# A table that also picks the engine of each copy, cast and sum, with forty SBUF sums on GpSimd

## The chip, the cores and the metric

The kernel runs on one core of a Trainium2 chip. The time is that of the device, in microseconds (us), from the start of the launch to its end; lower is better. Each version is run several times and the median is its time. A profile shows one execution. In it PE is the matrix engine (PEld is its loading of weights), DVE the vector engine, ACT the scalar engine, POOL is GpSimd, and SP is the engine that issues most of the DMAs (its queue is written SPq).

## The reference, cut to what matters

For 8 batches of 8 heads, 576 positions and 64 columns a head:

```python
def phi(x, c, s):
    r = np.maximum(x, 0.0)
    return np.concatenate([r * c, r * s], axis=-1)   # c, s: cos and sin of the position
q_p, k_p = phi(q, cos_w, sin_w), phi(k, cos_w, sin_w)
kv = np.einsum('bhsf,bhsd->bhfd', k_p, v)
z = np.sum(k_p, axis=2)
num = np.einsum('bhsf,bhfd->bhsd', q_p, kv)
den = np.einsum('bhsf,bhf->bhs', q_p, z)[..., None] + 1e-06
x = (num / den)            # heads side by side: 4608 rows of 512
h = x @ w_in               # 512 x 2048
g = h * np.cos(h)
out = g @ w_out            # 2048 x 512
```

All inputs and the output are float32; inside, the kernel computes its matrix products on float16 operands and sums them in float32.

## The kernel before, in words

**Work.** The 576 positions of a batch are handled as 512 rows plus a rest of 64. The eight 512-row parts and a ninth chunk made of the eight rests go through the two layers as nine chunks (`c` = 0 to 8). For each batch the attention stage runs: `load` brings k, q and v (two DMAs each from SP's queue); `prep` makes the cosine and sine features of q and k from float32 data in SBUF (`KQ<-km`, `KQ<-qm`, L452 on ACT, L453 on DVE); `cast_v` rounds v to float16 (`V<-vm`, L466 on ACT, L467 on DVE, L468 on POOL); `kv` multiplies (`ATT<-V,KQ`, L479) and copies the result to `kvz`; `num` multiplies with q (L542) and divides (L566, L568) into `x16`; and x is turned over into `xT`, by matrix products and a copy (`x_pe`, L588, L593) for the first three batches and by a transposing DMA (`x_dma`, L599) for the others. q is turned over in the same two ways (`q_pe`, L509, L514, L516, and `q_dma`, L520).

**Layers.** `layer1` computes h in PSUM banks, and `gate` evicts it: ACT takes the cosine (`ch<-M`, L609), DVE multiplies it with h into `gT` (L614). `layer2` makes the output rows in `ost`, which `store` writes out. From chunk 3 on part of layer 1, and from chunk 1 on all of layer 2, use a block scheme with seven half-size products in place of eight. That scheme needs **sums and differences of float16 blocks that lie in SBUF**: of the weights (`w_in_sums`, `WS`, L717; `w_out_sums`, `T`, L904), of x (`layer1_sums`, `XS`, L738) and of g (`layer2`, `S2`, `S3` and two updates in place of `gT`, L926 and L979). Its copies out of PSUM are `seed` (L663, bank to bank), `copy` in `layer1_fast` (`Z<-M`, L789), `copy` in `layer2` (`ost<-M`, L959) and one in `layer2_plain` (L889). In `layer1_fast` the gate of two blocks at once is a 1024-wide product of two float32 operands in SBUF (`gT<-Z,ch`, L808).

**Order.** Every operation is a step of `Plan`, with an engine, a cost, and the buffers that it reads and writes. The order in which each engine's steps stand is set by a list scheduler (`forward`) that takes one number per step from the table `KEYS`; the numbers are keys of order, not times. Steps with several possible engines (`either`: the features, the casts of v from batch 2 on, `den`) take the engine that is free first in the scheduler's account. Steps marked `port=True` on DVE and all on POOL are kept apart there. On the chip only data dependencies (semaphores) order the engines against each other.

**Start.** SP loads q, k and v of batch 0. POOL waits for k with a tiny cast (`hold`, L1027), then issues four DMAs for `w_in` (512 columns of the 2048 each, cast to float16 on the way), then those for `w_out`. The loads of batch 1 are held back: `hold_raw` (L1052) writes one element of each raw tile from an element of `w_in_sb`, named by `GATE1`, so that SP's load of k waits until that quarter of `w_in` has landed. `warm` (L1022) are products without use that keep PE's clock up while data are on the way.

Of the kernel before, what the change touches and what calls it, by code (L numbers as in the profile page):

```python
# [10 lines left out]
AF = mybir.ActivationFunctionType  # L11
# [6 lines left out]
    5824, 5995, 5824, 2967, 2673, 126, 143, -359, -2881, 263, -1072, -2121, 539, -49, 2962,  # L18
    2726, 3623, 3679, 1739, 3937, 2137, -2208, -6512, 4069, -2017, 702, -6077, -768, 703, -754,
    -6331, 8159, 3076, -1894, -5732, 1581, -6769, -1234, -877, -673, -882, -751, -1585, -1235,  # L20
    617, -63, -2524, -424, -626, 4458, 1519, -1459, -1432, 1518, -1601, 1517, -828, -5827,
    -6392, 1404, 4308, -2500, 2020, -1958, -2107, -3266, -4898, 8136, -5552, -8420, -2791,
    -1468, -4655, -1451, -1052, 783, -6576, 2792, -3465, -355, -8421, -3123, 6479, -3015, -6472,
    -1591, -2075, -2619, -2729, -7369, -6796, 3263, 798, -2481, 6480, -2003, -7073, 6781, 423,
    1982, 1241, 120, -9188, 1380, 643, -11779, -6829, 9984, -8175, -7566, 1246, -8162, 512,
    -312, -11302, 511, 10443, -10259, 2437, 605, 4807, 1897, 5905, -9831, -5057, 9984, 2301,
    -5301, 8846, -10101, -6662, 9020, -11634, -568, 7671, 5055, -1712, 6604, 584, 1196, 5001,
    -1672, 2279, 3129, 2596, 3289, 895, 532, -4417, -5551, -4542, 2044, 1687, 2846, 2800, 1902,
    3378, 993, -5427, 6673, -5442, 8455, 6488, 5906, 5871, 7397, -1850, 7157, -1228, 5182, 5994,
    7349, -880, 4039, 6762, 7533, 1736, 4177, 11737, 11954, 7479, 6368, 6930, 8684, 7392, 5307,  # L30
    17180, 16483, 5398, 7497, -1619, 7409, 8721, -161, 1062, -838, 10292, 5065, 5035, 7002,
    2938, 4999, 14973, 16942, 5320, 7491, 5034, 4630, 11782, 14974, 11886, 4631, 7315, 4601,
    4503, -692, -956, 4504, 7814, 2937, 3132, -860, 16897, -3069, -418, 10427, 3570, 3895, 4526,
    811, 1495, 8147, 4216, 8205, 4347, 7685, 6163, 8521, 4575, 8538, 4733, 3460, 8421, 9350,
    4611, 8493, 5428, 5849, 9131, 9146, 7933, 8134, 4534, 8052, 5570, 6030, 5703, 3236, 9273,
    5079, 7033, 7959, -732, 8555, 4350, -5307, 8046, 8768, 11196, 7765, 7621, 12926, 8253, 8411,
    11956, 11554, 8883, 13897, 9078, 9732, 12216, 1417, 8512, 13854, 7780, 9806, 6177, 5415,
    9049, -520, 5974, 11813, -2437, 5998, 8827, 10404, 7711, 13087, 3521, 9257, 1171, 1138,
    4633, 11805, 2569, 2323, 2261, 2582, 5745, 6182, 8706, 9578, 5077, 10082, 8860, -990, 8453,
    8541, 6221, 8499, 9036, 12232, 10067, 9664, 8544, 14012, 6360, 6188, 8015, 4438, -1489,  # L40
    6985, 8390, 5805, 5879, 5943, 6028, 8049, 8537, 10462, 5198, 8396, 8395, 12558, 4688, 9262,
    6122, 9046, 8189, 3466, 1589, 7820, 11893, 7819, 12664, 3857, 3643, 11985, 9433, 9054, 9210,
    8708, 8410, 9843, 8144, 4689, 8846, 8992, 9753, 8959, 11174, 12280, 10511, 11156, 9526,
    5553, 7072, 10317, 10402, 10261, 8357, 10403, 10051, 10267, 14404, 18351, 12204, 11240,
    9232, 9255, 18421, 14144, 12777, 11783, 7045, 11215, 9090, 7849, 7075, 9381, 10740, 5609,
    9483, 3041, 12189, 10009, 6763, 11687, 7171, 11186, 8968, 9229, 5228, 8069, 10107, 13655,
    8182, 10208, 13199, 8613, 9303, 15205, 7902, 9952, 15535, 6395, 9744, 4204, 6896, 8110,
    15935, 5192, 9656, 15578, 5752, 11091, 9533, 7831, 11765, 13714, 4074, 11936, 4217, 2177,
    4612, 7204, 2638, 7978, 7784, 4545, 8636, 6647, 6639, 5918, 8225, 3758, 5656, 6600, 8239,
    8692, 9382, 5468, 10740, 10372, 5666, 8703, 3916, 8802, 9066, 9050, 9298, 9304, 4801, 9527,  # L50
    9521, 8286, 11521, 9621, 9449, 6022, 5622, 9514, 9669, 10572, 6135, 8767, 7485, 8972, 9413,
    9995, 4213, 8900, 10075, 9675, 10273, 6234, 14794, 10195, 8079, 8885, 4804, 11145, 9576,
    11000, 9480, 10532, 11021, 11980, 10074, 11419, 13188, 13339, 10446, 11020, 12065, 12937,
    12270, 12793, 12994, 13467, 14479, 13933, 13146, 11684, 12054, 13603, 13106, 11695, 11512,
    14005, 13771, 13161, 15965, 16177, 16249, 16753, 13045, 12409, 18114, 13650, 12372, 12951,
    11343, 17252, 18836, 11725, 9919, 9604, 12293, 15415, 7956, 11448, 14519, 12454, 13519,
    14769, 15313, 12053, 13106, 13257, 13105, 13291, 11473, 11759, 13416, 11450, 13716, 18849,
    11925, 12834, 16093, 13478, 14576, 16431, 12255, 12362, 15960, 13160, 14519, 15910, 14407,
    11420, 14173, 9926, 10508, 15133, 9344, 13280, 12367, 9947, 9788, 14407, 10518, 12980,
    11697, 11766, 15535, 11429, 11430, 11395, 14648, 15418, 12373, 10069, 8755, 10521, 8003,  # L60
    11441, 13572, 10404, 12329, 17053, 10754, 11091, 10405, 4849, 9215, 7332, 8545, 10442, 9859,
    10283, 8824, 11855, 11042, 10408, 9428, 9240, 10089, 6840, 10015, 11937, 13432, 12329,
    14986, 8570, 13601, 11278, 9846, 10850, 12123, 10120, 9231, 12906, 11502, 11095, 17486,
    13263, 10990, 10503, 12334, 12434, 12727, 10556, 12848, 11321, 12810, 13349, 12759, 11144,
    9468, 12544, 13893, 13417, 10912, 9663, 12457, 8909, 13137, 14576, 14577, 13435, 14151,
    10310, 14092, 13571, 10884, 9832, 16768, 15657, 11596, 15684, 17182, 16270, 13098, 17070,
    15987, 15606, 6694, 19176, 16271, 6282, 21578, 15029, 12700, 14864, 23503, 25176, 13602,
    15549, 15974, 10832, 14466, 16061, 14589, 10209, 12007, 14031, 13538, 17903, 15093, 14046,
    16754, 11592, 18103, 14972, 15838, 14550, 15534, 14971, 15051, 13097, 12823, 12047, 14361,
    15045, 11016, 15607, 13066, 17291, 15370, 14684, 17730, 15344, 15696, 14507, 15369, 21381,  # L70
    12422, 13612, 16306, 16082, 6980, 15110, 25709, 16196, 6566, 16377, 16411, 13784, 6718,
    14056, 16929, 17039, 16412, 6717, 14282, 13875, 16186, 15098, 22414, 15303, 22094, 16880,
    22547, 17762, 13257, 17979, 16921, 14246, 17264, 11458, 9954, 12478, 12363, 11239, 12491,
    14328, 14703, 14327, 12412, 12275, 11391, 10099, 13674, 8800, 17476, 13817, 17651, 13961,
    11696, 6628, 12348, 11074, 13449, 15450, 13381, 15669, 12970, 15927, 14201, 13093, 13364,
    12833, 18387, 16087, 14472, 14480, 15193, 14959, 15363, 15351, 15446, 6483, 6363, 15673,
    13288, 19922, 16059, 5627, 15685, 13188, 12766, 16307, 5411, 15687, 15666, 15185, 16308,
    22136, 16271, 16582, 24827, 15769, 13994, 13943, 25782, 17223, 13256, 21089, 14718, 11697,
    19012, 23721, 13825, 12713, 16047, 27330, 19676, 26392, 12356, 19171, 19137, 25153, 20300,
    24575, 20816, 24148, 19933, 18704, 24601, 25241, 17614, 17642, 17213, 18192, 16667, 17540,  # L80
    17171, 17978, 15747, 16040, 12652, 16869, 17381, 18358, 12108, 26009, 16442, 15097, 18968,
    22506, 14325, 14468, 23722, 18748, 14353, 20959, 15309, 13207, 22948, 15406, 18806, 26434,
    17307, 19122, 13503, 14496, 16600, 16449, 18225, 17438, 15143, 16606, 15242, 16591, 19935,
    16631, 20110, 9977, 20151, 16345, 17596, 21986, 16007, 17814, 13492, 12529, 20878, 14542,
    9673, 17980, 17287, 16452, 14758, 16015, 17852, 17506, 19481, 13918, 17894, 12836, 13589,
    13910, 13566, 13751, 13668, 14062, 15321, 15434, 16469, 13488, 16029, 15409, 14091, 15728,
    14680, 15600, 16039, 16251, 16182, 25040, 25175, 15758, 15758, 15924, 19149, 16297, 17009,
    15666, 18342, 17524, 13007, 17309, 17010, 16166, 17102, 17420, 15086, 22399, 17317, 15221,
    17973, 25853, 16870, 21058, 13956, 17170, 22819, 13269, 14811, 19018, 17792, 25500, 20349,
    16959, 18873, 20325, 20305, 21587, 16184, 24900, 24202, 15971, 17496, 19642, 20403, 16741,  # L90
    21754, 22533, 22239, 10620, 21802, 21987, 17248, 21696, 21441, 23431, 22029, 23368, 17736,
# [1107 lines left out]
```

## Time and profile before

| | before |
|---|---|
| median of 3 runs | 285.55 us (285.11, 286.81, 285.55) |
| the profiled execution | 284.34 us, of which 282.3 us are its span, first to last instruction |
| granted PE clock | 0.993 |
| PE busy | 270.5 us, 2715 products |
| DVE busy | 249.2 us, 443 instructions |
| ACT busy | 218.0 us, 396 instructions |
| POOL busy | 19.2 us, 32 instructions |

"Busy" of PE covers the pipelined products from start to modelled end, so that a busy PE is not a proof that none was late; the distance from one start to the next tells that. The chain of waits lists, in order of time, what ran on the path that ended last: start, length, engine, tile, line and count. A line of the timeline gives start, length, engine, line, operation, tiles, shapes and count, and in brackets the idle time before it and what ended it. A line of the groups ends with count, busy time and mean nanoseconds of one.

### The profile page before, as it was taken

The numbers are of one execution on the slowest core, as the hardware profiler recorded it, in microseconds if no ns is written. First come the engines' busy times: TensorE is split into PE (matmuls) and PEld (weight loads), VectorE is DVE, ScalarE is ACT, GpSimd is POOL, SyncE is SP. The second block draws the span as 40 slices with busy tenths as digits, with TensorE's granted clock in tenths as the row PEclk, the third lists the DMA queues.
The fourth block names the chain that finished last, engine by engine and source line by source line (L and its number), as shares of the span: only waits on it lengthen the run. The fifth ranks groups of instructions, "written<-read, shape, count | busy, mean of one in ns | idle before, by whom it ended". The sixth has DMA issues, their size and how long they took to land.

```text
span 282.3 us, 6870 instructions
## 1 busy us (share of the span) xinstructions
PE 270.5 (96%) x2715; PEld 219.1 (78%) x2715; DVE 249.2 (88%) x443; ACT 218.0 (77%) x396; POOL 19.2 (7%) x32
## 2 busy tenths in 40 slices
PE   7799988999989999999999999999999999999994
PEld 2668956678967667779787988898788888888883
DVE  2877796999999989998999999999999999997952
ACT  2856698896899998599899999996676675877420
POOL 1440020010000010003003000210000000000000
PEclk9799999999999999999999999999999999999999
DMA  6999999969979999997999899988013100300124
GB/s 204 312 200 222 298 291 267 320 133 285 311 231 235 211 229 293 241 310 161 308 234 268 167 275 270 240 117 251 3 37 116 57 2 0 151 0 2 74 77 149
DMA packets 77599, 53.30 MB, mean 189 GB/s; under 512 B 46080, under 2 KB 75264, under 8 KB 77568
## 3 DMA queue, kind: packets, MB, share of 16 engines
q1 hardware_dynamic: 72608, 48.12, 66.7%
q0 software_dynamic: 4224, 4.19, 9.5%
q10 hardware_dynamic: 736, 0.57, 0.6%
q8 instruction: 21, 0.34, 0.5%
q14 instruction: 10, 0.08, 0.1%
HBM read 36.74 MB, written 9.44 MB: 164 GB/s over the span
## 4 chain that ended last, share of the span: by engine, by line
PE 85%; DVE 5%; DMA 4%; ACT 3%; issue 1%; DVEq 0%
PE M L948 32%; PE M L780 15%; PE M L637 10%; PE M L677 7%; PE TR L780 6%; PE M L880 5%; PE ATT L542 3%; DMA xT<-x 2%; PE ATT L479 2%; DMA qm<-in_q_dram 2%; PE M L509 2%; PE ATT L1022 1%; PE TR L677 1%; DVE x L568 1%; ACT xT L593 1%; ACT KQ L452 1%
## 5 line engine op out<-in xcount | busy, mean ns | idle before, releaser
L609 ACT ACTIVATE ch<-M 128x512 f32<-128x512 f32 x90 | 53.3, 597 | 14.4 <-PE M L637 6.9
L614 DVE TENSOR_TENSOR gT<-M,ch 128x512 f16<-128x512 f32 x84 | 56.7, 685 | 5.0 <-ACT ch L609 4.6
L948 PEld LDWEIGHTS <-gT 128*128 128x128 f16 x560 | 54.0, 98 | 7.6 <-DVE gT L926 0.5
L948 PE MATMUL M<-w_out_sb,gT 128*128 128x256 f16 x448 | 55.9, 273 | 0.0
L452 ACT ACTIVATE KQ<-km,CS 128x512 f16<-128x512 f32 x55 | 37.2, 715 | 0.2 <-DMA km<-in_k_dram 0.2
L452 ACT ACTIVATE KQ<-qm,CS 128x512 f16<-128x512 f32 x47 | 32.3, 721 | 4.5 <-DMA qm<-in_q_dram 4.5
L780 PEld LDWEIGHTS <-w_in_sb 128*128 128x128 f16 x320 | 30.8, 98 | 4.3 <-issue 0.2
L948 PE MATMUL M<-T,S 128*128 128x256 f16 x256 | 32.4, 273 | 0.0
L637 PE MATMUL M<-xT,w_in_sb 128*128 128x256 f16 x256 | 30.2, 273 | 0.1
L677 PE MATMUL M<-xT,w_in_sb 128*128 128x512 f16 x112 | 27.6, 379 | 0.8 <-ACT xT L593 0.8
L948 PEld LDWEIGHTS <-S 128*128 128x128 f16 x256 | 24.7, 98 | 4.0 <-issue 0.2
L637 PEld LDWEIGHTS <-w_in_sb 128*128 128x128 f16 x256 | 24.5, 98 | 3.5 <-issue 0.4
L568 DVE TENSOR_TENSOR x<-ATT,rec 128x512 f16<-128x512 f32 x32 | 22.1, 692 | 2.3
L959 ACT ACTIVATE ost<-M 128x512 f32<-128x512 f32 x24 | 14.1, 593 | 12.1 <-PE M L948 9.3
L780 PEld LDWEIGHTS <-WS 128*128 128x128 f16 x216 | 20.5, 98 | 3.3 <-issue 0.5
L677 PEld LDWEIGHTS <-w_in_sb 128*128 128x128 f16 x128 | 12.2, 98 | 10.8 <-issue 0.9
L453 DVE TENSOR_SCALAR KQ<-qm,CS 128x512 f16<-128x512 f32 x33 | 15.4, 498 | 5.1 <-DMA qm<-in_q_dram 5.1
L468 POOL CAST V<-vm 128x1024 f16<-128x1024 f32 (+1 forms) x11 | 10.7, 1004 | 134.9 <-PE M L948 46.0
L542 PEld LDWEIGHTS <-qT 128*128 128x128 f16 x320 | 15.3, 98 | 4.6 <-issue 1.8
L926 DVE TENSOR_TENSOR S<-gT 128x2048 f16<-128x2048 f16 (+1 forms) x16 | 17.4, 1085 | 0.2
L808 DVE TENSOR_TENSOR gT<-Z,ch 128x1024 f16<-128x1024 f32 x13 | 15.9, 1221 | 0.7 <-ACT ch L802 0.4
L542 PE MATMUL ATT<-kvz,qT 128*128 128x65 f16 x288 | 15.7, 194 | 0.6 <-DVE x L568 0.5
(135 smaller groups left out, 461.3 us busy)
## 6 DMA issues: line engine op xcount, KB each, us to landing
out_dram<-ost SPq DMA_DIRECT2D x33, 256.0 KB, 3.0
qm<-in_q_dram SPq DMA_DIRECT2D x8, 640.0 KB, 5.9
km<-in_k_dram SPq DMA_DIRECT2D x8, 640.0 KB, 5.6
qm<-in_q_dram SPq DMA_DIRECT2D x8, 512.0 KB, 6.2
km<-in_k_dram SPq DMA_DIRECT2D x8, 512.0 KB, 5.7
vm<-in_v_dram SPq DMA_DIRECT2D x6, 640.0 KB, 7.2
vm<-in_v_dram SPq DMA_DIRECT2D x6, 512.0 KB, 6.5
w_in_sb<-in_moe_w_in_dram POOLq DMA_DIRECT2D x4, 512.0 KB, 8.9
```

What stands on the lines that cost most here:

```text
L452: fn = {"ACT": lambda: nc.scalar.activation(out=out_, in_=in_, func=AF.Relu, scale=sc), "DVE": lambda: nc.vector.tensor_scalar(out=out_, i ...
L453: "DVE": lambda: nc.vector.tensor_scalar(out=out_, in0=in_, scalar1=0.0, scalar2=sc, op0=ALU.max, op1=ALU.mult)}
L542: nc.tensor.matmul(bank[hb][:, hh * D1:(hh + 1) * D1], lhsT=a[:, h, :], rhs=z[:, h, :], start=(i == 0), stop=(i == len(parts) - 1))
L568: nc.vector.tensor_tensor(out=split(x16[n][:, hs, :], k), in0=A[:, :, :, 0:D], in1=split(rec[n][:, hs], k).unsqueeze(3).broadcast_to((P, k ...
L609: act(0.5, due, lambda: nc.scalar.activation(out=ch[c], in_=bank, func=AF.Sin, bias=math.pi / 2.0, scale=1.0), [key], [("ch", c)])
L614: dve(0.61, due, lambda: nc.vector.tensor_tensor(out=dst, in0=a, in1=b, op=ALU.mult), [key, ("ch", c), *rd], dkeys)
L637: nc.tensor.matmul(M1[m][:, jj * 2 * P:(jj + 1) * 2 * P], lhsT=w_in_sb[:, cc, j * P:(j + 1) * P], rhs=X[:, cc, ts], start=(cc == 0), stop= ...
L677: nc.tensor.matmul(M, lhsT=w_in_sb[:, cc, j * P:(j + 1) * P], rhs=X[:, cc, :], start=(cc == 0), stop=(cc == NCT - 1))
L780: nc.tensor.matmul(bank[0][:, j * TH:(j + 1) * TH], lhsT=a(cc, j), rhs=b[:, cc, :], start=(first and j == 0 and cc == 0), stop=(last and j ...
L808: dve(1.14, due, lambda: nc.vector.tensor_tensor(out=g4, in0=four(uz), in1=four(cc2), op=ALU.mult), zk + ck, [("g", gi(c), h * JH + j, t) ...
L926: dve(0.07 + 1.07 / NG, due, lambda: nc.vector.tensor_tensor(out=out_[:, sl], in0=a[:, sl], in1=b[:, sl], op=op), rd, wr, port=True)
L948: nc.tensor.matmul(bank[0][:, tt * MH:(tt + 1) * MH], lhsT=a[:, j, tt * P:(tt + 1) * P], rhs=b[:, j, :], start=(first and (apart or tt == ...
```

## The change

Each entry of `KEYS` now carries two things: the last digit picks the engine of the step (0: as before, the one free first; n: the n-th of its engines), the rest is the key of order. Copies out of PSUM may go to ACT or DVE (`copies`), the sums of SBUF blocks and the 1024-wide product L808 to DVE or POOL (`sums`). All entries of the table are new, so the order on every engine changes as well. `GATE1` names the first quarter of `w_in` in place of the third.

```diff
 KEYS = (
-    5824, 5995, 5824, 2967, 2673, 126, 143, -359, ...
+    -171000, -168830, -137080, 10080, -69160, -86640, ...
 )
 def run(self):
-        start, done = self.forward([k / 100 for k in KEYS])
+        for s, k in zip(st, KEYS):
+            self.pick(s, k % 10)
+        start, done = self.forward([k // 10 / 100 for k in KEYS])
+    def pick(self, s, i):
+        if i:
+            e = list(s["opts"])[i - 1]
+            s["opts"] = {e: s["opts"][e]}
...
-    GATE1 = (w_in_sb[0:2, 0, Dff // 2 + 1:Dff // 2 + 2], [("w_in", 2)])
+    GATE1 = (w_in_sb[0:2, 0, 1:2], [("w_in", 0)])
...
+    def copies(due, cost, out_, in_, rd, wr, hint):
+        either(due, cost, {
+            "ACT": lambda: nc.scalar.activation(out=out_, in_=in_, func=AF.Copy),
+            "DVE": lambda: nc.vector.tensor_copy(out=out_, in_=in_)}, rd, wr, hint, port=False)
+
+    def sums(due, n, out_, in0, in1, op, rd, wr, lazy=None, rate=0.523e-3):
+        def go(q):
+            return lambda: q.tensor_tensor(out=out_, in0=in0, in1=in1, op=op)
+        either(due, {"DVE": 0.07 + n * rate, "POOL": 0.05 + n * 2.05e-3},
+               {"DVE": go(nc.vector), "POOL": go(nc.gpsimd)}, rd, wr, 1, lazy=lazy)
...
     # seed, copy in layer1_fast and layer2, layer2_plain, kv, q_pe, x_pe, the same way:
-        act(0.5, due, lambda: nc.scalar.activation(out=dst[0], in_=bank[0], func=AF.Copy),
-            [bank[1]], [dst[1]])
+        copies(due, {"ACT": 0.5, "DVE": 0.61}, dst[0], bank[0], [bank[1]], [dst[1]], 1)
...
     # w_in_sums, layer1_sums, out2 (L808), w_out_sums, layer2, the same way:
-                dve(0.07 + 1.07 / NG, due, lambda: nc.vector.tensor_tensor(
-                    out=out_[:, sl], in0=a[:, sl], in1=b[:, sl], op=op), rd, wr, port=True)
+                sums(due, JH * TH // NG, out_[:, sl], a[:, sl], b[:, sl], op, rd, wr)
```

What the table makes of it, counted in the built programs:

| | before | after |
|---|---|---|
| SBUF sums of two float16 blocks on DVE: 512, 1024, 2048 wide | 40, 16, 28 | 15, 11, 22 |
| the same on POOL | none | 25, 5, 6 |
| products of two float32 operands, 1024 wide (L808): DVE, POOL | 20, 0 | 16, 4 |
| copies 512 wide out of PSUM, float32: ACT, DVE | 104, 0 | 81, 23 |
| the same to float16 (L593): ACT, DVE | 13, 0 | 11, 2 |
| features (L452 on ACT, L453 on DVE) | 102, 58 | 93, 67 |
| casts of v, 1024 wide: DVE, POOL | 3, 9 | 0, 12 |

PE has the same 2715 products, in another order in places. In the order of POOL an instruction that is no computation (it reloads the library of GpSimd's code) stands once, ahead of the first sum; the program before has none. The four DMAs of `w_in` stand in the order first, second, third, fourth quarter, before it was first, third, second, fourth; of the first two quarters of `w_out` the second is now issued first, and between the two issues stands the hold that SP's load of batch 1's k waits for.

## The prediction

> **What bounds the kernel now.** I read the page first: busy shares, then the slices.
>
> ```profile
> PE 270.5 (96%) x2715; PEld 219.1 (78%) x2715; DVE 249.2 (88%) x443; ACT 218.0 (77%) x396; POOL 19.2 (7%) x32
> PE   7799988999989999999999999999999999999994
> DVE  2877796999999989998999999999999999997952
> ```
>
> PE bounds it, and busy PE is nearly all useful: adding the shortest start-to-start distance of each shape over all 2715 products (216 ns for 512 columns, 109 for 256, 56 for 128, 29 for 65) gives 262.4 us. The first product starts at 1.3, the last ends at 278.0; PE loses only 12.8 us against that sum in gaps between starts, 6.75 before 20 us (q, k and w_in still arriving), 5.9 after. The change touches no product, so 5.9 us plus some of the head is all that it can earn. The waits of PE and the chain tell where these 5.9 lie.
>
> ```profile
> PE ATT L479 <- DVE V L467: 1.2, 1, 1.2
> PE M L677 <- ACT xT L593: 0.8, 1, 0.8
> PE ATT L542 <- DVE x L568: 0.5, 1, 0.5
> PE M L780 <- DVE XS L738: 0.3, 1, 0.3
> ```
> ```profile
> 40.42 0.69 DVE qT L516
> 41.98 0.72 ACT V L466 x2
> 42.70 0.61 ACT KQ L452
> 43.31 0.91 ACT qT L514
> 44.22 0.62 ACT KQ L452
> ...
> 99.36 6.57 DMA xT<-x
> 106.03 0.74 DVE XS L738
> ```
>
> By starts: 2.7 us at 40.8 to 46 (kv of batch 1), 0.9 at 79.5 (xT), 0.5 at 107.5 (XS), 0.7 at 113.3 (x), 0.5 at 20 to 24, 0.7 in crumbs from 143 on. From 120 us PE never rests, and DVE hardly:
>
> ```profile
> 120.00:130.00 10.00, 10.00 (x98) 8.26 (x96) 9.41 (x19) 9.84 (x20) 1.60 (x2) 1.00 1.01 265
> ```
>
> Between 120 and 270 us DVE is idle for 6.3 of 150.
>
> **The sums on POOL.** 40 of them go from DVE to POOL, 34,304 elements a partition. DVE is relieved of 25 x 0.415 + 5 x 0.69 + 6 x 1.215 + 4 x 1.222 = 26.0 us. It gets 23 copies out of PSUM in float32 (no such row; its product with PSUM, L614, took 0.685, so 15.8), two for xT (1.2) and 9 features (0.478 each, 4.3), and loses three casts (2.1): about 7 us less in all. ACT loses 23 x 0.597, 2 x 0.6 and 9 x 0.716, some 21 us, and has 65 to spare already, so that earns nothing by itself. POOL never added two tensors in this trace; its nearest row is the cast, one operand in, one out:
>
> ```profile
> L468 POOL CAST V<-vm 128x1024 f16<-128x1024 f32 x9 | 9.7, 1088 | 134.9 <-PE M L948 46.0 <-DMA vm<-in_v_dram 40.6 <-PE M L677 26.9
> L926 DVE TENSOR_TENSOR S<-gT 128x2048 f16<-128x2048 f16 x12 | 14.6, 1217 | 0.1
> ```
>
> At 1.04 ns an element, the sums take 36 us if the second operand is free, 71 if it doubles the price, 107 at three passes. I take 71, the middle (512: 1.1 us, 1024: 2.2, 2048: 4.3), because a second operand is the one thing that the cast lacks. With 15 us of casts POOL is then busy some 87 us of 282: a free engine, if the sums are ready early. The Trainium skill's GPSIMD Engine Reference, section 3.1, gives 4497 ns for such a sum of 2048 float32 elements, by which the 40 would take an estimated 75 us. No run here shows it.
>
> PE feels a sum only through its latest reader. In the built order the first reader of a sum stands 3 to 12 us of PE's work behind it; closest are the XS sums of chunks 3, 5 and 6, some half a dozen with about 2.5. The first, S3 of chunk 1, has most at stake: before, DVE did it at 68.1, and the next instruction that waits for it is DVE's update of gT at 81.67, so that 81.7 - (68.1 + 4.3) = 9.3 us also cover POOL's library reload ahead of it.
>
> **POOL against DVE.** The trace shows a price that no semaphore orders:
>
> ```profile
> 57.38 1.05 POOL L468 CAST V<-vm 128x1024 f16<-128x1024 f32 x1 [18.71 <-DMA vm<-in_v_dram]
> ```
> ```profile
> 104.45 2.05 POOL L468 CAST V<-vm 128x1024 f16<-128x1024 f32 x2 [46.02 <-PE M L948]
> 106.03 0.74 DVE L738 TENSOR_TENSOR XS<-xT 128x512 f16<-128x512 f16 x1 [0.80 <-DMA xT<-x]
> ```
>
> The XS sum took 0.74 in place of 0.41 and ended 0.27 after the second cast; the DVE feature at 58.05 took 0.66 in place of 0.478 beside the cast of 57.38. Two more stretch so, 1.0 us over 11 casts. DVE's products with an operand in PSUM keep their 0.685 beside casts. If DVE's SBUF-only instructions fell on POOL's at random and each waited the rest out, the casts would have cost about 3.7 us (a cast meets 0.8 starts a us of such instructions before 120 us and 0.55 after, each times half of 1.06 squared); 1.0 was seen, 0.27 of it, since the order keeps them apart. From 120 to 270 us the changed order has 61 SBUF-only instructions on DVE and on POOL 5 sums of 2048, 8 of 1024, 15 of 512 and 4 casts, about 60 us. At random they would cost 61 x (5 x 4.3² + 8 x 2.2² + 15 x 1.1² + 4 x 1.06²) / (2 x 150) = 31 us; at 0.27, 8.4. DVE's spare there is 6.3 plus what it sheds in this stretch (off: 5 x 1.215, 3 x 1.22, 5 x 0.69, 15 x 0.415, or 19.4; on: 18 copies x 0.685 and 7 features x 0.478, or 15.7), 10.0 us. So 8.4 is covered, and is 0 in the sum; without that cover it is the second rival. The Trainium skill's SBUF — State Buffer, section Who interferes with whom, says that a DVE instruction with two SBUF inputs contends with a GpSimd one that reads SBUF, and that the later of the two blocks for the whole instruction; the 0.74 agrees, and its full blocking is the "at random" end.
>
> **kv of batch 1.** Before, the last two K features ran on ACT at 41.4 and 42.7, behind and between the casts of V, and PE waited 2.7 us. Now all K features stand ahead of the casts, and GATE1 opens SP's load of k with the first landing of w_in (17.6 against 20.3 for the second; through the holds and one DMA issue of 0.75 the load starts about 19.5 against 20.74), with k_1's rest, q, v and w_out queued behind it. v landed at 39.0 to 41.3, with DMA saturated until 56 us, so an earlier issue hardly moves it: 41.3 plus a cast of 0.7 leaves PE half its wait. Saved: 1.3, bounds 0 to 2.5. Head and w_in products before that: 0 (the first quarters still land 17.6 to 26.0, in an order that suits the products as before; bounds -0.5 to 0.5).
>
> **The moved products.** Ahead of L677 of chunk 2 PE now has transposes of batch 1's x and 1.75 us of L948 that stood behind; they cover the wait of 79.5: 0.9 (0 to 0.92). Batch 3's first L780 and its sums stand 1.6 to 2.6 us later: 0.8 of the 1.16 at 107 and 113 (0 to 1.16). Crumbs: 0.3 (0 to 0.7), as DVE is a little freer. Against it: batch 3's V casts go from DVE (0.7 each) to POOL, 2 x 1.06 one after the other, while V landed at 80.4 and kv starts at 84.8, and half a dozen sums of 1.1 us on POOL are close to their readers: 0.3 lost (0 to 1.7). The tail from 276 us has the same last additions and stores: 0.
>
> **Sum.** -1.3 - 0.9 - 0.8 - 0.3 + 0.3 = -3.0 against the profiled 284.34 (span 282.3 and 2.04 around it). That execution is 1.2 below the median 285.55; I carry the difference over: 282.5 us. The least possible is 285.55 - 5.9 = 279.7.
>
> **Rivals.**
> *No difference.* kv of batch 1 still waits for v, which DMA brings at 41.3 whatever the gate does, and the chunk-2 and batch-3 waits reappear at the next reader, since ACT copies xT and DVE divides x at the same pace. For it: DMA 0.9 and more until 56 us. Against: K features, not v, ended the last 2 us of that wait. It would gain 1: 284.5.
> *Slower: the shared access of POOL and DVE.* The price is the 31 us above, and it decides from a share of 10/31 = 0.32 (seen: 0.27, near). At two thirds, 21 - 10 = 11 over: 293.5; from (10 + 5.9)/31 = 0.51 it is over 1% slower. For it: a sum on POOL is four times as long as a cast and may drift, since nothing but the planned order keeps it off. One place: in layer2 the 4.3 us update of gT can start while DVE still has a feature and an L808 product ahead. Against: in DVE's built order 29 of the 40 sums are followed by at least their own length of work with an operand in PSUM.
> *Slower: the library reload.* One instruction of POOL that the trace of before lacks. Above 9 us it holds L926 and through it PE; 20 us would give 282.5 + 11 = 293. No row bears on its length. The GPSIMD reference, section 2.1, tells of about 6 us for a first call into freshly loaded code, by which the cover suffices.
>
> **How the numbers follow.** Forecast 0.53 (its own range 280.2 to 284), no difference 0.25, shared access 0.18, reload 0.04. A difference of 1%, 2.86 us, is about what a measurement of this kernel can tell from none: 282.69 and 288.41 are the bounds. The forecast stands right at the first; with crumbs and kv on the good side more often than not, 0.42 of its 0.53 falls beyond. Same: 0.11 + 0.25 + 0.02 of the shared-access case = 0.38. Slower: 0.16 + 0.04 = 0.20. The range goes from the floor, 279.8, to 291, a share of 0.6 for the rival; what lies above, most of reload and half of the rival, is about 0.14.
>
> **What would show it.** Right: POOL's sums at about 1.1, 2.2 and 4.3 us; DVE's SBUF sums still near 0.415, 0.69 and 1.215 on the mean; DVE busy some 242 and ACT 197 us; the wait of L479 on V below 0.7, no wait of L677 on xT, L780's on XS gone. Wrong: means of DVE's SBUF-only rows well up (2048 at 1.6 or more), with L614 late and PE waiting for gT or ost after 120 us (the first rival); a hole of PE at 75 to 90 us with POOL idle ahead of its first sum (reload); the 40 to 46 us wait unchanged, ended by V (no difference). POOL at three passes would make the half-dozen close sums late by half a us each, and the forecast wrong by some 3.

## The result, and the profile after

The changed kernel took 289.88 us (median of 4; 288.96 to 293.94) against 285.59 us before: a ratio of 1.0133, 95% interval 1.0087 to 1.0179. I had forecast 282.5. In the experiments the same kernel was run again on another occasion (E0) and took 292.88 us, ratio 1.0256 (1.0197 to 1.0315); the profile of that run (292.31 us, span 290.5) is read here, because the profiled execution of the first measurement was its slowest and not typical. In the changed program the sums stand in line 447, the features in 488 (ACT) and 489 (DVE), the gate's product in 643 (before: 614), layer 1's products in 666, 705 and 808 (637, 677, 780), layer 2's in 907 and 972 (880, 948).

The page, busy shares and slices, as shown for the kernel before:

```profile
PE 272.9 (94%) x2715; PEld 218.4 (75%) x2715; DVE 255.0 (88%) x430; ACT 202.2 (70%) x365; POOL 103.9 (36%) x76
PE   6899999999999996999977999999999899999994
DVE  2978888998998997997997999999999999988972
```

PE has three dents that it had not, in slice 16, in 21 and 22, and in 32 (a slice is 7.3 us). DVE was to lose some 7 us of work and is 6 us busier. What PE waits for:

```profile
PE M L808 <- DVE gT L643: 4.4, 4, 2.8
PE TR L705 <- DVE gT L643: 3.5, 1, 3.5
PE M L907 <- DMA w_out_sb<-in_moe_w_out_dram: 0.7, 1, 0.7
```

The old waits (V for L479, xT, XS, x) are gone or small; in their place stands the gate's product of DVE, twice for about 3 us. From start to start PE loses 21.0 us in place of 12.8, and the span grew by the same 8.2. The timeline of DVE and POOL ahead of the 3.5 us wait:

```profile
147.23 1.22 DVE L447 TENSOR_TENSOR S<-gT 128x2048 f16<-128x2048 f16 x1
148.37 0.48 DVE L489 TENSOR_SCALAR KQ<-qm,CS 128x512 f16<-128x512 f32 x1
148.60 4.17 POOL L447 TENSOR_TENSOR gT<-gT,S 128x2048 f16<-128x2048 f16 x1 [2.66 <-DVE S L447]
148.77 5.08 DVE L447 TENSOR_TENSOR gT<-Z,ch 128x1024 f16<-128x1024 f32 x1
...
153.77 0.68 DVE L643 TENSOR_TENSOR gT<-TR,ch 128x512 f16<-128x512 f32 x1
```

This is the loss in five lines. DVE's product gT<-Z,ch takes 1.22 us when it is alone. POOL's update started 0.17 us ahead of it and ran to 152.77; DVE's ended at 153.85, 1.08 later: it stood still for the whole of POOL's instruction and then did its own work. Behind it in DVE's queue stood the gate's product L643 that PE needed for a free bank.

The other place is a row of six short sums on POOL beside six SBUF-only instructions of DVE:

```profile
103.76 1.37 DVE L489 TENSOR_SCALAR KQ<-qm,CS 128x512 f16<-128x512 f32 x1
104.81 1.33 POOL L447 TENSOR_TENSOR WS<-w_in_sb 128x512 f16<-128x512 f16 x1
105.05 2.17 DVE L447 TENSOR_TENSOR S<-gT 128x2048 f16<-128x2048 f16 x1
105.12 0.60 PE L808 MATMUL M<-xT,w_in_sb 128*128 128x256 f16 x4
106.22 2.01 POOL L447 TENSOR_TENSOR w_in_sb<-w_in_sb 128x512 f16<-128x512 f16 x1
107.15 0.68 DVE L643 TENSOR_TENSOR gT<-M,ch 128x512 f16<-128x512 f32 x1
```

Here the two engines take turns: each waits for the other to end, the feature takes 1.37 in place of 0.48, the 2048-wide sum 2.17 in place of 1.22, POOL's own sums 2.0 in place of 1.15. The product with an operand in PSUM keeps its 0.68. I compared each instruction of DVE that starts after 50 us with the median of its operation and shape in the kernel before, and call the excess its stretch: 17 are stretched, by 13.8 us in all (before: 4, by 1.0), and each of them lies beside work of POOL. (The expectations below give 13.6 and 14 us for the changed kernel and 11.7 for E7; counted this way the first profile has 14.2 and E7 18.7.) The groups show it as means, two of the kernel before and then three of E0 (the 2048-wide sum took 1217 ns before):

```profile
L453 DVE TENSOR_SCALAR KQ<-qm,CS 128x512 f16<-128x512 f32 x33 | 15.4, 498 | 5.1 <-DMA qm<-in_q_dram 5.1
L808 DVE TENSOR_TENSOR gT<-Z,ch 128x1024 f16<-128x1024 f32 x13 | 15.9, 1221 | 0.7 <-ACT ch L802 0.4
```

```profile
L489 DVE TENSOR_SCALAR KQ<-qm,CS 128x512 f16<-128x512 f32 x35 | 19.1, 582 | 4.9 <-DMA qm<-in_q_dram 4.9
L447 DVE TENSOR_TENSOR gT<-Z,ch 128x1024 f16<-128x1024 f32 x11 | 17.3, 1573 | 0.4 <-ACT ch L830 0.4
L447 DVE TENSOR_TENSOR S<-gT 128x2048 f16<-128x2048 f16 x9 | 12.8, 1417 | 0.1
```

### The profile page after: what moved, and what is told of

Its sections match the earlier page's. It is cut to its first block, busy times and chain, and to the rows that moved or that the text cites. A ratio compares the mean times of both kernels' runs of the same rounds, so it can differ in the third digit from the quotient of the medians.

```text
span 292.2 us, 6908 instructions
## 1 busy us (share of the span) xinstructions
PE 274.5 (94%) x2715; PEld 218.8 (75%) x2715; DVE 255.6 (87%) x430; ACT 202.3 (69%) x365; POOL 104.9 (36%) x76
## 4 chain that ended last, share of the span: by engine, by line
PE 59%; DVE 17%; DMA 14%; issue 3%; POOL 2%; ACT 2%; SPq 1%; DVEq 0%; POOLq 0%; ACTq 0%
PE M L972 26%; PE M L808 14%; PE M L705 6%; DMA qm<-in_q_dram 5%; PE TR L808 5%; DMA w_out_sb<-in_moe_w_out_dram 4%; DVE gT L447 4%; DVE KQ L489 3%; PE M L666 3%; DVE gT L643 3%; DMA km<-in_k_dram 3%; PE ATT L574 2%; DMA w_in_sb<-in_moe_w_in_dram 2%; PE ATT L515 2%; DVE S L447 1%
## 5 line engine op out<-in xcount | busy, mean ns | idle before, releaser
L643 DVE TENSOR_TENSOR gT<-M,ch 128x512 f16<-128x512 f32 x84 | 56.0, 684 | 3.3 <-ACT ch L638 3.1
L808 PEld LDWEIGHTS <-w_in_sb 128*128 128x128 f16 x320 | 30.7, 98 | 9.9 <-DVE gT L643 3.3
L488 ACT ACTIVATE KQ<-qm,CS 128x512 f16<-128x512 f32 x45 | 30.2, 715 | 4.2 <-DMA qm<-in_q_dram 4.2
L488 ACT ACTIVATE KQ<-km,CS 128x512 f16<-128x512 f32 x48 | 32.7, 717 | 0.3 <-DMA km<-in_k_dram 0.3
L504 POOL CAST V<-vm 128x1024 f16<-128x1024 f32 (+1 forms) x15 | 16.6, 1143 | 44.1 <-DMA vm<-in_v_dram 32.4
L705 PE MATMUL M<-xT,w_in_sb 128*128 128x512 f16 x112 | 28.5, 388 | 0.0
L489 DVE TENSOR_SCALAR KQ<-qm,CS 128x512 f16<-128x512 f32 x35 | 19.6, 597 | 4.9 <-DMA qm<-in_q_dram 4.9
L808 PEld LDWEIGHTS <-WS 128*128 128x128 f16 x216 | 21.2, 100 | 3.3 <-issue 0.6
L447 POOL TENSOR_TENSOR S<-gT 128x2048 f16<-128x2048 f16 (+1 forms) x5 | 16.5, 3294 | 12.3 <-DVE den L594 9.1
L830 ACT ACTIVATE ch<-Z 128x1024 f32<-128x1024 f32 x14 | 14.7, 1052 | 6.3 <-DVE Z L821 6.1
L447 POOL TENSOR_TENSOR gT<-gT,S 128x2048 f16<-128x2048 f16 (+1 forms) x4 | 15.4, 3840 | 9.2 <-DVE S L447 9.2
```

The source lines that it names most:

```text
L447: return lambda: q.tensor_tensor(out=out_, in0=in0, in1=in1, op=op)
L488: fn = {"ACT": lambda: nc.scalar.activation(out=out_, in_=in_, func=AF.Relu, scale=sc), "DVE": lambda: nc.vector.tensor_scalar(out=out_, i ...
L489: "DVE": lambda: nc.vector.tensor_scalar(out=out_, in0=in_, scalar1=0.0, scalar2=sc, op0=ALU.max, op1=ALU.mult)}
L504: "POOL": lambda: nc.gpsimd.tensor_copy(out=out_, in_=in_)}
L643: dve(0.61, due, lambda: nc.vector.tensor_tensor(out=dst, in0=a, in1=b, op=ALU.mult), [key, ("ch", c), *rd], dkeys)
L705: nc.tensor.matmul(M, lhsT=w_in_sb[:, cc, j * P:(j + 1) * P], rhs=X[:, cc, :], start=(cc == 0), stop=(cc == NCT - 1))
```

## The experiments

Three theories stood against each other. Theory 1, shared access: DVE's SBUF-only instructions stand still while POOL reads SBUF. Theory 2, late sums: POOL takes two to three times as long for a sum, and the readers wait. Theory 3: the new order and DVE's new copies cost the time. In all variants "at its place" means that the step keeps its position in the order and only its engine differs. The edits are shown shortened, some of them in words.

**E0, the changed kernel again.**

> The changed kernel once more, for a profile to read beside the others. All theories: about 289.6 us. Theory 1 (shared access: a DVE instruction whose operands all lie in SBUF stands still while POOL works on SBUF operands): the same places as in the first profile, DVE's L808 product near 150 us at about 5.1 us in place of 1.22, the DVE work beside the eight or so POOL sums at 104 to 113 us stretched by some 4 us, two layer-2 sums at 230 us by 0.85 us each, 13.6 us of stretch in all. If the stretches fall at other places from run to run, the order is not what makes them.

292.88 us, 3.3 above what I expected. The stretches beside sums fell on the same instructions (3.86 us at the L808 product both times, 3.95 and 4.12 in the row at 103 to 112, twice 0.85 at 228 to 232); those beside casts before 80 us vary (0.80 and 0.46 here, 0.61, 0.79 and 0.06 in the first profile). The order makes the former, not chance.

**E1, one sum moved.** `on_pool` is the list of the 40 sums in order.

```diff
+        on_pool[16]["fn"] = on_pool[16]["all"]["DVE"][3]     # gT<-gT,S at 149 us
```

> One instruction of the changed kernel moved: the 2048-wide update gT<-gT,S that POOL starts at 150.2 us goes to DVE, at the same place of the order; the other 39 sums stay on POOL. Theory 1 (shared access): DVE's L808 product behind it falls from 5.08 to 1.22 us, DVE pays 1.22 for the sum, and most of PE's 3.6 us wait for gT at 152.5 goes: 286 to 287.5 us. Theory 2 (POOL's sums come late to their readers because they take 2.8 to 3.5 times as long): PE reads this one about 8 us later and nobody waits for it, so no change, or up to 1.2 slower, as DVE has more to do: 289.6 to 290.8. Theory 3 (the new order and the copies on DVE cost the time): as theory 2.

286.92 us, ratio 1.0059 (1.0022 to 1.0096): 6.0 us below E0 for one instruction moved. The product gT<-Z,ch falls to 1.22, and PE's hole at 151 us from 3.64 to 0.91. The drop is more than I expected. In the profiles the hole accounts for 2.7 us of it and PE's half clock behind that hole for 1.7; another 1.3 is the half clock behind the hole at 108 us, which E1 lacks. That hole lies ahead of the moved sum, so this part is luck (last section). Theories 2 and 3 had no gain here.

**E2, the order alone.**

```diff
+        for s in on_pool: s["fn"] = s["all"]["DVE"][3]
+        for s in order:
+            if s is a copy out of PSUM: s["fn"] = its engine in the kernel before
```

> The changed kernel's order kept, but all 40 sums back on DVE and the 25 moved copies back on ACT, each at its place in the order (features, casts of v, GATE1 stay as changed). Theory 1 (shared access): no stretch is left but beside casts (below 2 us); DVE is about as busy as in the kernel before (250 us); kv of batch 1 and the moved products keep their gain of 2 to 3 us, some of it lost since the order was made for other engines: 283 to 286 us. Theory 2 (late sums): the same, 283 to 286. Theory 3 (order and copies): the order is still there, so 288 or more.

294.73 us, ratio 1.0308 (1.0248 to 1.0368): a miss of mine. Without POOL's sums only 1.0 us of stretch is left, and still it is slower than E0. There is no large hole; from 130 us on PE loses 10.9 us in pieces of up to 1 us, on gT, x, Z and ost from DVE and ACT. The order was drawn up for a DVE without those sums; that this is the reason is my reading and was not tested by itself. What E2 shows is that the order gains nothing on the old engines. It doesn't explain E1, and E3, E5 and E6 below keep both the new order and the copies on DVE and are faster than the kernel before.

**E3, write only.**

```diff
-            q.tensor_tensor(out=out_, in0=in0, in1=in1, op=op)          # on POOL
+            q.tensor_tensor(out=few(out_), in0=few(in0), in1=few(in1), op=op)   # one element in 64
+            for _ in range(2):
+                q.memset(out_, 0.0)
```

> The changed kernel with each of POOL's 40 sums replaced by a sum of one element in 64 (it waits for the same inputs) and two fills of the whole output with a constant, which read nothing and take about as long as the sum took (512 wide: two times 0.53 us, 2048: two times 2.1). It leaves out the sums' values. POOL is as busy and its results are as late as in the changed kernel, but it hardly reads SBUF. Theory 1 in the form that the reads collide: DVE's rows fall back to 0.478 (features), 1.22 (L808 and 2048-wide sums), the waits of PE at 109, 152 and 233 us go, and the time is near what I forecast, 282 to 284.5 us. If writes block as well, it stays at 288 to 291. Theory 2 (late sums): POOL's outputs come as late as before, 288.5 to 290.5. Theory 3: as theory 2.

281.75 us, ratio 0.9854 (0.9790 to 0.9919), 11 us below E0. The same place as above:

```profile
144.58 0.48 DVE L501 TENSOR_SCALAR KQ<-qm,CS 128x512 f16<-128x512 f32 x1
144.80 0.46 POOL L457 TENSOR_TENSOR gT<-gT,S 128x32 f16<-128x32 f16 x1 [1.98 <-DVE S L451]
144.97 1.32 DVE L451 TENSOR_TENSOR gT<-Z,ch 128x1024 f16<-128x1024 f32 x1
145.33 3.67 POOL L459 MEMSET gT<- 128x2048 f16 x2
```

POOL is at work for 4.1 us as before and its result is as late, but the product of DVE takes 1.32, beside fills that only write. POOL is as busy (102.7 us) and DVE's stretch falls to 2.0 us. Theory 1 alone forecast this, and the time is a little below its 282 to 284.5. The kernel leaves out the sums' values, so it shows the cause and is no version to use. The Trainium skill, SBUF — State Buffer, section Who interferes with whom, says that a DVE instruction with two SBUF inputs contends with a GpSimd one that reads SBUF but not with one that only writes it: the 5.08 and the 1.32 agree with both halves. Fills are not free for every instruction, though: beside fills alone no sum or L808 product in E3 and E11 was stretched by more than about 0.1 us, but five of seven features were (0.60 to 0.97 us in place of 0.478).

**E4, two steps swapped.** In the scheduler's account POOL's update follows the L808 product; on the chip it waits only for S2.

```diff
-    order on DVE:  S2, feature, gT<-Z,ch      (POOL's gT<-gT,S waits for S2)
+    order on DVE:  feature, gT<-Z,ch, S2
```

> All engines as changed; one DVE sum moved in the order. In the order of the changed kernel DVE does S2, a feature and the L808 product, and POOL's update gT<-gT,S was planned behind that product; but on the chip it waits only for S2 and so starts 0.2 us ahead of the product. Here S2 stands behind the product, so that POOL cannot start before it. No work changes engine, none is added. Theory 1 (shared access, decided by who starts first): the product falls from 5.08 to 1.22 us, the wait of PE at 151 us goes, and with it the half clock behind it: 286 to 287.5 us, as with the sum on DVE. If the sum's length on POOL were the point, it would now end 1.7 us later and the time would stay at 292 to 293.

287.58 us, ratio 1.0076 (1.0028 to 1.0124). All engines and all work are those of E0; POOL's update now starts at 149.31, behind the product, which takes 1.22. Who starts first decides, and the time cannot be told from E1's.

**E5, fences.**

```diff
+    def behind(ap, fn):                       # ap: result of the last SBUF-only step of DVE
+        nc.gpsimd.tensor_copy(out=mark, in_=one element of ap)
+        fn()                                  # POOL's sum
```

> The changed kernel with a copy of one element on POOL ahead of each of its 40 sums, which reads the result of the last SBUF-only instruction that stands ahead of it in DVE's order: so POOL's sums can't start before that instruction, as the order was planned. It adds 40 short copies to POOL (some 0.2 us each). Theory 1: where a sum got ahead of the planned place (150 us, parts of 104 to 113 and of 228 to 232 us) the stretch goes, of 14 us some 6 to 9; POOL's sums come later instead, some late for PE: 284 to 289 us. If nothing got ahead of its place, the time stays at 292 or more.

282.89 us, ratio 0.9925 (0.9891 to 0.9959): faster than both kernels and than the 284 to 289 that I expected, with all 40 sums on POOL.

```profile
147.06 1.22 DVE L468 TENSOR_TENSOR gT<-Z,ch 128x1024 f16<-128x1024 f32 x1
148.41 0.18 POOL L437 COPY mark<-gT 1x1 f16<-1x1 f16 x1 [4.18 <-DVE gT L468]
148.55 4.05 POOL L468 TENSOR_TENSOR gT<-gT,S 128x2048 f16<-128x2048 f16 x1
152.78 0.48 DVE L511 TENSOR_SCALAR KQ<-km,CS 128x512 f16<-128x512 f32 x1
```

The short copy waits for the product, the sum of 4.05 us follows, and DVE's next SBUF-only instruction starts 0.18 us after its end: DVE's order had PSUM work for just this stretch, as planned. The stretch is 6.5 us in place of 13.8. So the plan was right at this place, and the scheduler's account wasn't binding on the chip.

**E6, ten sums back on DVE.**

```diff
+        for i in (5, 6, 7, 8, 9, 10, 16, 29, 30, 31): on_pool[i]["fn"] = on_pool[i]["all"]["DVE"][3]
```

> The ten sums on POOL that stretch DVE most (six at 102 to 112 us, the update at 149 us, three at 228 to 233 us) go back to DVE, each at its place in the order; 30 stay on POOL. DVE is given 9 x 0.415 + 1.22 = 5.0 us and loses some 10 of the 14 us of stretch. Theory 1: no wait of PE for gT at 108, 151 and 231 us, no half clock behind them; 283 to 285 us, no slower than the kernel before. If it was DVE's load that counted and not the stretch, 290 or more.

283.77 us, ratio 0.9958 (0.9920 to 0.9995). DVE has 5.0 us more to do and the time falls by 9.1 against E0: not DVE's load, but the standing still.

**E7, the order before with the 40 sums on POOL, and E11, the same with write-only sums.**

```diff
-                s["fn"]()
+                s["fn"](nc.gpsimd) if s["n"] in ON_POOL else s["fn"]()
```

> The kernel before with its order kept and the same 40 sums on POOL: nothing of the new table but the engine of the sums. Nothing in this order keeps POOL's sums apart from DVE's SBUF-only work. Theory 1: stretches at many places, 20 us or more (my estimate for starts at random was 31 us from 120 us on), holes of PE behind the long ones: 293 to 305 us. Theory 2 (late sums): PE's waits on POOL's XS, S and WS at the end, DVE's rows unstretched; also slower, 290 or more. If neither, the relief of DVE would show: 283 to 286.

> The kernel before with its order and the same 40 sums on POOL (305.0 us), each replaced as in the write-only run: a sum of one element in 64, which waits for the inputs, and two fills as long as the sum. It leaves out the sums' values. The results are as late for their readers as in the 305.0 us version, but POOL hardly reads SBUF. Theory 1 (shared access) alone: the 11.7 us of stretch on DVE and the holes go, 286 to 290 us. Theory 2 (sums late for readers, in an order that was not made for POOL's lengths): the waits for XS, S and gT stay, 298 us or more. Both: between, and the difference to 305 is the share of shared access.

E7: 305.03 us, ratio 1.0695 (1.0623 to 1.0767). E11: 290.83 us, ratio 1.0233 (1.0150 to 1.0316). The stretch of DVE is 18.7 us in E7 and 3.1 in E11. Of the 20 us that the sums cost in an order that was not made for them, about 14 go with the reads; the other 6 stay with late sums (in E11 PE waits 3.9 us once for XS from DVE and 1.0 for XS from POOL). Theory 2 is real there. My 31 us for starts at random between 120 and 270 us were too many: E7 has 15.1 there, about half, in an order that knew nothing of POOL's sums.

**E8 to E10, variants of the fences.** E8 issues w_out's second DMA ahead of the hold of k, E9 puts fences ahead of the casts too, E10 gives six sums back to DVE.

> The version with fences, with one DMA issue moved on POOL's queue: the second of the first two w_out DMAs goes ahead of the hold that SP's load of batch 1's k waits for, as it stood in the kernel before. Tests whether the new start (GATE1) made w_out late: PE waited 0.9 to 1.6 us for w_out at 34.7 us in the changed kernel and with fences, and 0 in the kernel before. If the early load of k is what delays w_out, the wait goes, k starts 0.75 us later, and the time is 0.5 to 1.5 us below that with fences (282.9): 281.4 to 282.4. If DMA bandwidth alone sets both, it moves to kv of batch 1 and the time stays at 282.9.

> Fences ahead of POOL's casts of v as well as its sums. Theory 1 (shared access): the three stretches beside casts (58.5, 104 and 154.5 us, 1.7 us in all) shrink where the cast got ahead of its place; the casts may come late for kv, which follows them closely. 282 to 284 us: no better than fences on the sums alone unless the waits of PE for gT at 56 to 63 us (1.3 us) go with the first stretch, which would give 281.5.

> The version with fences, with the six sums of 102 to 117 us back on DVE at their places (34 stay on POOL). With fences these six, in the busiest stretch of DVE, still stretch DVE by 2.8 us and PE has 2.2 us of holes there (109 and 118.7 us); on DVE they cost 2.5 us and stretch nothing. Theory 1: the holes mostly go, 281.5 to 282.5 us. If DVE's load is what counts there, no gain: 283 to 284.

283.95, 283.01 and 283.42 us; ratios 0.9949 (0.9919 to 0.9979), 0.9921 (0.9886 to 0.9956) and 0.9947 (0.9918 to 0.9977). All beat the kernel before, none is to be told from E5. In E8 the wait for w_out went from 1.60 to 0.46 us and one of 1.32 for features of q came up at 38.6: moved, not gained, and my 281.4 to 282.4 was a miss. In E9 the holes between 56 and 63 us went and no others came, for which I had expected 281.5; its median says no more than E5's. E10 is a miss too: theory 1 had 281.5 to 282.5 for it, and 283.42 lies where I had put the rival, that DVE's load counts there. In its profile PE's losses between 100 and 120 us are gone (0.06 in place of 2.25 us), and from 120 us on they are 1.3 larger than in E5's.

## Why the prediction failed, by its own steps

**The failed step is "So 8.4 is covered, and is 0 in the sum".** The size came out: from 120 to 270 us E0 has stretches of 0.80, 0.35, 3.86, 0.09, 0.69, 0.87, 0.85, 0.84 and 0.27, 8.6 us. That is in part luck, as nearly half of it is one overlap, and without that one E1 has 4.5. The cover did not hold. I set 8.4 us of standing still against 10.0 us of idle time that lay scattered over 150 us. But 3.9 of it fell on one instruction, with the gate's product queued behind it, and PE's next product came 3.6 us late. Idle time of DVE elsewhere gave nothing back: DVE was still idle for 11.3 of these 150 us, while PE's loss there rose from 0.9 to 8.3 us. E1 and E4 show it: with that one overlap gone, DVE's sum of work being 1.2 us more or the same, 5 to 6 us were gained.

**The window was too narrow.** I summed from 120 us on. 3.95 us of stretch lie at 103 to 112, where DVE has no spare (0.3 us idle from 100 to 113): a hole of 2.98 us.

**The order alone does not keep the engines apart.** I carried the share of 0.27 over from the casts "since the order keeps them apart", and named, under the second rival, the very place where the update can start ahead of the feature and the L808 product. I then took it for one place among forty. E5 shows the difference between an order in an account and an order on the chip: 10 us. From 120 to 270 us the stretch is 15.1 us in E7's order, 8.6 in the new one and 2.9 in E5 with fences. The rival's mechanism is the one that happened. Its decision point was wrong for the same reason as the cover: the loss came at a share of 8.6/31 = 0.28, below 0.32. The size I gave the rival, 293.5, was for a share of two thirds; that it lies beside 289.9 and 292.9 is luck. Its sign, a mean of 1.6 us or more for the 2048-wide sums, did not come either (1.42): a mean hides the one instruction that counts. (The floor stands in the prediction as 279.7 and as 279.8; it is 285.55 - 5.9 = 279.65.)

**What held.** POOL's sums took 4.07, 2.13 and 1.15 us where undisturbed (4.3, 2.2 and 1.1 forecast): the second operand doubles the cast's price. DVE without its stretch would be busy 241.2 us (255.0 - 13.8; forecast 242), ACT is at 202 (197). The reload of POOL's library cost nothing that shows:

```profile
L447 POOL TENSOR_TENSOR S<-gT 128x2048 f16<-128x2048 f16 x3 | 12.2, 4066 | 12.2 <-DVE den L594 9.1 <-DVE gT L447 3.1
```

The 9.1 us of POOL's idle time ahead of the first sum ended with DVE's work, not with POOL's own; a reload shorter than that would not be seen. The waits for xT and XS went as forecast. kv of batch 1 gave 1.8 where 1.3 was forecast: between 40 and 50 us PE's loss fell from 2.71 to 0.87. But a new wait for w_out of 0.87 at 34.7 us, which the sum does not have, took half of that back.

**What the change is worth without the collision.** E3 gives -1.5% with writes alone, E5 -0.75% with fences. The 3.0 us that I forecast, 1.05%, lies between the two: a gain of that size is there for the new order and engines when POOL's reads do not block DVE, which the changed kernel doesn't see to. No run checks the terms of the sum one by one.

## What to carry to other kernels

Work that moves to GpSimd is not off DVE's path if it reads SBUF: here a DVE instruction with all its operands in SBUF waited for the end of GpSimd's, so weigh each pair by its place, by what is queued behind the blocked instruction and who waits for that, and never by a mean of idle time. A scheduler that keeps two engines apart must have a semaphore to do it; a copy of one element that reads the other engine's result was enough here (0.18 us each when undisturbed). Test one suspected overlap alone first: one instruction moved told more here than 40.

## What was not expected of the hardware

**PE's clock falls behind some holes of 3 us.** Windows of E0 around the 3.6 us hole, columns as in the prediction's window line, the granted clock third from the end:

```profile
151.00:153.00 2.00, 0.03 (x1) 0.00 (x0) 2.00 (x1) 0.00 (x0) 1.76 (x1) 1.00 1.09 346
153.00:155.00 2.00, 0.50 (x3) 0.26 (x3) 1.97 (x4) 1.12 (x3) 1.30 (x2) 1.00 0.57 127
155.00:157.00 2.00, 2.00 (x21) 1.35 (x20) 1.97 (x4) 2.00 (x5) 0.75 (x1) 0.50 0.26 51
157.00:159.00 2.00, 2.00 (x14) 1.51 (x12) 1.29 (x3) 0.88 (x2) 0.00 (x0) 0.65 0.11 23
```

For about 3.4 us (from 154.98 to 158.40) the 256-wide products start 0.21 us apart in place of 0.109, and PE loses another 1.65 us. The hole of 2.98 us at 108 us is followed by a clock of 0.50 too, 1.3 us lost; the hole of 2.92 at the same place in E1 and E4 is not (the line is of E1):

```profile
113.00:115.00 2.00, 2.00 (x20) 1.34 (x18) 1.90 (x5) 1.99 (x4) 0.10 (x1) 1.00 1.12 270
```

The size of the hole does not decide alone; its place does too. In all 14 profiles the granted clock changes on a grid of 3.41 us, whose position differs from execution to execution. After 20 us, wherever PE at full clock idled for 2.15 us or more of one cell of the grid, the clock behind that cell was 0.50; where it idled for 1.96 or less it stayed at 1.00. (In the first 10 us it is less clear: of cells with 1.76 to 1.92 us idle some were followed by 0.50 and some not.) E0's hole at 108 us puts 2.15 us into one cell (107.19 to 110.61). The holes of 2.92 in E1 and E4 lie across a border of the grid and put at most 1.61 and 1.96 us into one. So 1.3 of the 6 us that E1 gained come from where the grid lay. The Trainium skill, TensorE: Matmul & The Clock Gate, describes in section What's actually happening a free-running window of 3413 ns and an idle window as what halves the clock, and in section Why this matters for your kernels advises against idle gaps of PE over about 3 us; the grid agrees with the window, but a window need not be idle throughout: 2.15 of its 3.41 us were enough here.

It may also be part of why the same kernel took 289.9 us on one occasion and 292.9 on the other. The four executions of the first had mean granted clocks of 1.00, 1.00, 0.985 and 0.985 (288.96, 290.00, 289.76 and 293.94 us), those of E0 0.982 to 0.994 (292.3 to 293.9). The 289.76 at 0.985 does not fit, so the cause stays open.

**The standing still is mutual and whole.** DVE's 5.08 us are POOL's 4.17 less a head start of 0.17, and its own 1.1. POOL's copy of one element took 1.17 us in E5 beside a 2048-wide sum of DVE, and 0.18 alone. A feature, one SBUF operand and a column of scalars, is blocked like a sum; products with an operand in PSUM are not (683 ns over 84 of them, 685 before).
